# Weight preparation of experts 1 to 5 reordered in a chunked-attention, MoE and dense-MoE kernel

## Chip, cores and metric

The program runs on 1 core of one Trainium2 chip. The metric is device microseconds of one execution of the whole program, from its first to its last instruction. TensorE (PE in the profile) multiplies, VectorE (DVE), ScalarE (ACT) and GpSimd (POOL) do the element-wise work, SyncE (SP) issues most DMAs. Each engine takes its own instructions strictly in the order in which they were written; engines meet only at semaphores.

## What is computed

Three layers follow each other. Only the second, a top-1 mixture of experts, is touched by the change.

```python
attn_out = _attn_ref(**attn_kwargs)              # softmax(q k^T) v within chunks of 64
x = attn_out.transpose(0, 2, 1, 3).reshape(2304, 512)
x = _moe_ref(x=x, **moe_kwargs)                  # each token goes to one of 8 experts
return _moe2_ref(x=x, **moe2_kwargs)             # every token through 8 experts, weighted

# _moe_ref, per expert e, for the tokens routed to it (at most 576):
h = np.maximum(disp[e] @ w1[e], 0.0)             # w1[e] is 512 x 1024
y = h @ w2[e]                                    # w2[e] is 1024 x 512
out[i] = gate_w[i] * y[...]
```

## The kernel before

All matrices are split into two f16 parts, high and low, and each product is three f16 products: high by high, low by high, high by low. So a weight matrix must be prepared before it is used. For each expert that is, for w1 (called a, `nm == "a"`) and w2 (called b):

- **load**: four DMAs into a staging tile (`sta`, `stb`; two of each, used in turn by odd and even experts);
- **statistics** (`w_stat`): four quarters, by ScalarE squares with a running sum for a (line 168), by VectorE maxima for b (line 170);
- **total** (`w_scale`, line 177): one small matmul on TensorE over the partitions, which needs all four quarters;
- **scale** (`w_scale2`): some tiny VectorE instructions that turn the total into a power of two;
- **split** (`w_split`): four quarters each. ScalarE writes the high part (lines 246, 254). The low part comes from VectorE (line 255), or, for two quarters of b, from GpSimd in two steps (lines 247 and 248).

The experts of the first mixture run one after the other, x = 0 to 7. While expert x multiplies, the matrices of y = x + 1 get totals, scales and splits, and those of x + 2 get their loads and statistics. Nothing schedules this at run time: the order is written by hand. `blocks` runs one expert for up to 256 tokens:

- the first product in four groups of 24 matmuls (`first_product`, line 355). Behind each group, `hidden` takes it out of PSUM: ScalarE writes `hh` (line 360), VectorE writes `hl` (line 361). The groups take three PSUM banks in turn, so the fourth group waits until `hl` of the first is written;
- then two rows t = 0 and 1 (128 tokens each) of the second product, 24 matmuls each (line 975). Behind each, the **row finish**: ScalarE square (979), VectorE scale (89 to 92), ScalarE high part (985), VectorE low part (986) and factor (991), and two DMAs (990, 994).

`sites` is a list of six lists of steps. The first four stand behind the four groups, the fifth behind row 0's finish, the sixth behind row 1's finish. `behind` puts a step ahead of matmul step kk of a row (each of the 8 steps has 3 matmuls); at `(0, KF)`, behind row 0's last matmul, stands `late_turn`, which transposes 256 more tokens. After `blocks`, one or two **further blocks** of 128 tokens run, where the count of the expert is over 256 or over 384. In this input expert 2 has two, experts 3 and 6 have one, experts 1, 4 and 5 have none.

In the kernel before, expert 1 alone uses a late order: first total behind the third group, second total at kk = 4 of row 0, splits of b behind row 0's finish. Experts 2 to 6 make both totals and scales behind the first group and spread the eight splits over the four groups. In all of them the statistics of x + 2 (`stats`) stand in the fifth site, ahead of row 1's finish.

Of the kernel before, what the change touches and what calls it, by code (L numbers as in the profile page):

```python
# [30 lines left out]
def kernel(ctx, tc, q, k, v, w_gate, w1, w2, capacity, w2_gate, w21, w22, out):  # L31
# [3 lines left out]
    E, _, F = w1.shape  # L35
# [4 lines left out]
    KF = F // 128  # L40
# [109 lines left out]
    def w_load(x, nm, h, nh=2, behind_vector=False):  # L150
        if h == 0:
            w_new(x, nm)
        m = mats[x, nm]
        c = m.kk // nh
        if behind_vector:
            nc.vector.memset(m.st[:, h * c, 0:1], 0.0)
        nc.sync.dma_start(out=m.st[:, h * c:(h + 1) * c, :],
                          in_=m.src[h * c * 128:(h + 1) * c * 128, :].rearrange("(k p) n -> p k n", p=128))
# [145 lines left out]
    for i in range(NS):  # L304
        r, done = [], 0
        while done < 256:
            b, s = divmod(i * 256 + done, S)
# [600 lines left out]
    with ExitStack() as cctx:  # L908
# [19 lines left out]
        def turn_dma(rows):  # L928
            xT = cp.tile([128, 2 * KD, 256], F16, tag="xT", name="xT", bufs=2)
            for n, (idx, kg, xg) in enumerate(rows):  # L930
                nc.sync.dma_start_transpose(out=xT[:, :, n * 128:(n + 1) * 128], in_=xg)
            return xT, rows
# [70 lines left out]
        def load(x, nm, *hs):  # L1003
            return [lambda h=h: w_load(x, nm, h, 4, x == 2) for h in hs]
# [13 lines left out]
        def tokens(x, *ts):  # L1018
            return [gidx[:, x, t:t + 1] for t in ts]
# [74 lines left out]
        for x in range(E):  # L1094
            y = x + 1

            def skip(b):
                tc.mark_branch_hint_location(f"{b}{x}", rc > {"m": 256, "n": 384}[b], engines=[mybir.EngineType.PE])

            def count(of, counts=reg_i):  # L1100
                return nc.values_load(counts[0:1, of:of + 1], min_val=0, max_val=N)

            def next_count():
                if y < E:
                    counted_next.append(count(y))

            counted_next = []
            if x > 0:
                rc = rc_next
            rb = nc.values_load(reg_i[0:1, E + x:E + x + 1], engines=[mybir.EngineType.SP], min_val=0, max_val=N)  # L1110

            def rank(t):
                return nc.s_assert_within(rb + t * 128, 0, N + 128,
                                          skip_runtime_bounds_check_because="a block starts at most 128 past the last token")

            def ranks(t0):
                return lambda t: rb if t0 + t == 0 else rank(t0 + t)

            def rows_ahead():
                return gather(tokens(y, 2, 3)) if y < E else None, gather(tokens(y + 1, 0, 1)) if y + 1 < E else None  # L1120

            late_cur = late
            if x > 0:
                for f in load(x + 2, "b", 0, 1) if x + 2 < E else ():
                    f()
                cur, pre = pre, turn_dma(rows) if y < E else None
                late, rows = rows_ahead()
            if x == E - 1:
                with tc.If(rc <= N - SB):
                    heads(nc.sync)  # L1130

            if y < E:
                for nm in "ab":
                    w_alloc(y, nm)
                sp = [lambda h=h, nm=nm: w_split(y, nm, h, 4, 2 * (nm == "b" and h > 1)) for h, nm in
                      (((0, "a"), (2, "b"), (1, "a"), (2, "a"), (3, "b"), (3, "a"), (0, "b"), (1, "b")) if x > 1 else
                       ((0, "a"), (1, "a"), (2, "a"), (3, "a"), (2, "b"), (3, "b"), (0, "b"), (1, "b")))]
                sc = [lambda f=f, nm=nm: f(y, nm) for f in (w_scale, w_scale2) for nm in "ab"]
                steps = sc + sp
                counts = (6, 2, 2, 2)  # L1140
            else:
                w_alloc(E, "a")
                wsum = stage2.tile([128, 4, 4, 2, 128], F32, tag="stb", name="wsum")
                wsums += [wsum[:, i] for i in range(4)]
                for q in range(4):
                    w_quad(E, "a", q, 0)
                steps = [lambda f=f: f(E, "a") for f in (w_scale, w_scale2)] + [
                    lambda q=q, i=i: w_quad(E, "a", q, i) for q in range(4) for i in (1, 2)]
                counts = 4, 2, 2, 2
            sites = []  # L1150
            for n in counts:
                sites.append(steps[:n])
                steps = steps[n:]
            assert not steps
            second_sc, second_sp = [], []
            if x == 1:
                sites = [kept_stats[0:1], kept_stats[1:2], [sc[0], sc[2], kept_stats[2], sp[0]], [*sp[1:4], kept_stats[3]]]
                second_sc, second_sp = [sc[1], sc[3]], sp[4:]
            if 0 < x < E - 2:
                sites[1] += load(x + 2, "b", 2, 3)  # L1160
            later = load(x + 3, "a", 0, 1, 2, 3) if x + 3 <= E else []
            stats = []
            for h in range(4):
                if x + 2 <= E:
                    stats.append(lambda h=h: w_stat(x + 2, "a", h, True))
                if x + 2 < E:
                    stats.append(lambda h=h: w_stat(x + 2, "b", h, False))
                elif x == E - 1:
                    sites[h].append(lambda h=h: w_stat(E, "b", h, True))
            nxt = []  # L1170

            def late_turn():
                if x > 0:
                    nxt.append(turn(late_cur, "xTc", "p"))
                    return
                turn_into(e_xT, late_cur, "y")
                for j in range(2):
                    nc.vector.tensor_copy(l_kg[:, j:j + 1], l_rows[j][:, DM:DM + 1])
                nxt.append((e_xT, late_cur))

            if x == 0:
                ahead = []
                every = [f for part in sites for f in part]
                la, lb = load(2, "a", 0, 1, 2, 3), load(2, "b", 0, 1, 2, 3)
                pre_next = turn_dma(rows)
                for f in [every[0], every[2], every[4], every[5]]:
                    f()
                blocks(x, pre, 2, ranks(0), [[*la, lambda: ahead.append(rows_ahead())], lb],
                       True, behind={(0, KF): late_turn})
                pre = pre_next  # L1190
                late, rows = ahead[0]
            else:
                sites += [second_sp + later[:2] + stats if x != E - 2 else load(E, "b", 0, 1, 2, 3) + stats, later[2:]]
                sites[3].append(lambda: skip("m"))
                sites[4].append(next_count)
                blocks(x, cur, 2, ranks(0), sites, True,
                       behind={(0, 4): lambda: [f() for f in second_sc], (0, KF): late_turn})
            late_t, late_r = nxt[0]

            def further(t, sites=()):  # L1200
                blocks(x, (late_t[:, :, (t - 2) * 128:(t - 1) * 128], late_r[t - 2:t - 1]), 1, lambda _: rank(t), sites)

            if x == 0:
                blocks(x, nxt[0], 2, ranks(2), [
                    [lambda: more.append(count(0, e_any)), next_stats[0]], [next_stats[1]], next_stats[2:], [next_count],
                    every[9:],
                    [lambda: tc.mark_branch_hint_location("r", more[0] > 512, engines=[mybir.EngineType.PE]), *later, *stats[0::2]]],
                    behind={(0, 3): lambda: (every[1](), every[3]()), (0, 4): every[6], (0, 5): every[7], (0, 6): every[8]})
                kept_stats = [lambda h=h: w_stat(2, "b", h, False) for h in range(4)]
            else:  # L1210
                with tc.If(rc > 256, label=f"m{x}"):
                    further(2, [[lambda: skip("n")], [], []])
                    with tc.If(rc > 384, label=f"n{x}"):
                        further(3)
            if x == 0:
                with tc.If(more[0] > 512, label="r"):
                    whole()
            if y < E:
                rc_next = counted_next[0]
            else:  # L1220
                with tc.If(rc > N - SB):
                    heads(nc.gpsimd)
# [524 lines left out]
```

## Time and profile before

| | us |
|---|---|
| median of 3 runs | 1748.15 |
| lowest and highest | 1746.42, 1748.84 |
| the profiled execution | 1746.32 |
| span in its profile | 1744.6 |
| experts 1 to 6 within the span | 161.7 to 360.8 |

The profiled execution lies 1.83 us below the median and 1.72 us above its span. The first mixture is about an eighth of the span; the attention lies ahead of it and the second mixture, over two thirds of the span, behind it. The page gives the busy time of each engine; tables by stretch show it per expert, and the waits and timelines show what each engine waited for and when. Times in the timelines count from the start of the span.

### The profile page before, as it was taken

How to read it: one execution, taken by the hardware profiler on the slowest of the kernel's cores; microseconds unless marked ns; L12 is line 12 of the kernel's file. 1: busy time of each engine (PE TensorE's matmuls, PEld its weight loads, DVE VectorE, ACT ScalarE, POOL GpSimd, SP SyncE). 2: the span in 40 equal slices, each digit the busy share in tenths (PEclk: the TensorE clock that was granted, in tenths of full speed). 3: DMA queues.
4: the chain of work that ended last, by engine and by line, in shares of the span. 5: the costliest groups of instructions: out<-in, count | busy, mean ns of one | idle time of the engine just before them, and what ended most of it. 6: DMA issues, size and time to landing. Idle time of an engine off the chain costs nothing.

```text
span 1744.6 us, 33605 instructions
## 1 busy us (share of the span) xinstructions
PE 1695.6 (97%) x13323; PEld 1233.2 (71%) x13323; DVE 1191.8 (68%) x2313; ACT 946.9 (54%) x1795; POOL 715.7 (41%) x758
## 2 busy tenths in 40 slices
PE   8999799989999999999999999999999999999998
PEld 7876466666545577777777777777777777777776
DVE  6886767856567766786677767667766686677554
ACT  6866656764445654665355545555644565364431
POOL 2225544632021333553355444453534543454433
PEclk9999899999999999999999999999999999999999
DMA  9948868845253313242233224223323141323201
GB/s 223 238 137 248 234 162 187 222 116 140 82 148 107 136 62 133 64 175 71 105 116 131 99 95 151 106 85 112 127 92 133 64 171 47 134 64 127 91 35 49
DMA packets 140766, 219.08 MB, mean 126 GB/s; under 512 B 62656, under 2 KB 81120, under 8 KB 140592
## 3 DMA queue, kind: packets, MB, share of 16 engines
q1 hardware_dynamic: 135440, 200.00, 36.6%
q0 software_dynamic: 5152, 16.72, 3.6%
q8 instruction: 114, 1.87, 0.4%
q14 instruction: 60, 0.49, 0.1%
HBM read 167.56 MB, written 41.91 MB: 120 GB/s over the span
## 4 chain that ended last, share of the span: by engine, by line
PE 66%; DVE 6%; ACT 2%; issue 1%; DMA 1%; POOL 1%; SPq 1%; POOLq 0%; DVEq 0%; ACTq 0%
PE p_m L1437 35%; PE p_m L1533 27%; PE p_m L1581 4%; DVE wall L297 3%; ACT wall L296 1%; DVE acc L1504 1%; DMA wb_d<-wall 1%; SPq L1272 1%; PE p_m L1325 0%; DVE xsum L1286 0%; ACT eh L1442 0%; POOL out_dram L1515 0%; DMA x<-x_d 0%; DVE el L1445 0%; ACT tq L1477 0%
## 5 line engine op out<-in xcount | busy, mean ns | idle before, releaser
L1437 PE MATMUL p_m<-x,wall 128*128 128x384 f16 x4032 | 666.9, 326 | 6.0 <-ACT tq L1477 5.1
L1437 PEld LDWEIGHTS <-wall 128*128 128x128 f16 x4032 | 394.1, 98 | 263.4 <-issue 8.8
L1533 PE MATMUL p_m<-wall,eh 128*128 128x256 f16 x3528 | 580.3, 273 | 0.0
L1449 POOL TENSOR_TENSOR el<-tq,eh 128x384 f16<-128x384 f32 x336 | 347.2, 1061 | 560.1 <-ACT eh L1442 559.8
L1533 PE MATMUL p_m<-wall,el 128*128 128x256 f16 x1764 | 480.8, 273 | 0.0
L1442 ACT ACTIVATE eh<-tq 128x384 f16<-128x384 f32 x540 | 274.1, 522 | 189.8 <-DVE tq L1455 101.4
L1533 PEld LDWEIGHTS <-eh 128*128 128x128 f16 x3528 | 344.3, 98 | 44.4
L1504 DVE SCALAR_TENSOR_TENSOR acc<-p_m,cf,acc 128x256 f32<-128x256 f32 (+1 forms) x378 | 175.6, 521 | 130.3 <-PE p_m L1533 129.8
L1452 DVE TENSOR_TENSOR tq<-p_m,tq 128x384 f32<-128x384 f32 x288 | 158.5, 556 | 125.7 <-PE p_m L1437 124.6
L1533 PEld LDWEIGHTS <-el 128*128 128x128 f16 x1764 | 172.6, 98 | 19.9
L1445 DVE SCALAR_TENSOR_TENSOR el<-tq,eh 128x384 f16<-128x384 f32 x204 | 175.1, 860 | 10.0 <-ACT eh L1442 8.6
L1455 DVE SCALAR_TENSOR_TENSOR tq<-tq 128x384 f32<-128x384 f32 x252 | 133.2, 553 | 2.9
L355 PEld LDWEIGHTS <-wall 128*128 128x128 f16 x1248 | 107.2, 99 | 19.6 <-issue 5.4
L1477 ACT COPY tq<-p_m 128x384 f32<-128x384 f32 x96 | 45.7, 476 | 110.6 <-PE p_m L1437 108.2
L247 POOL TENSOR_SCALAR stb<-stb,wsb 128x1024 f32<-128x1024 f32 x16 | 52.7, 3291 | 81.2 <-DVE tq L1452 46.8
L1581 PE MATMUL p_m<-wall,eh 128*128 128x512 f16 x288 | 85.6, 379 | 0.0
L275 POOL TENSOR_TENSOR tq<-stb 128x256 f32<-128x256 f32 x56 | 48.7, 870 | 82.2 <-DVE wsumsq L184 58.9
L296 ACT ACTIVATE wall<-stb,wsb 128x256 f16<-128x256 f32 (+1 forms) x56 | 31.3, 605 | 93.3 <-DMA wb_d<-wall 67.9
L1490 ACT ACTIVATE tq<-tq 128x384 f32<-128x384 f32 x84 | 43.9, 522 | 70.0 <-DVE tq L1452 70.0
L355 PE MATMUL p_p<-xT,wall 128*128 128x256 f16 x672 | 77.6, 276 | 3.6 <-DMA rk_d<-rkt 1.2
L275 POOL TENSOR_TENSOR tq<-sta 128x256 f32<-128x256 f32 x56 | 43.5, 777 | 83.3 <-DVE wall L297 48.6
L297 DVE SCALAR_TENSOR_TENSOR wall<-stb,wsb,wall 128x256 f16<-128x256 f32 (+1 forms) x56 | 38.5, 698 | 48.3 <-ACT wall L296 45.8
(288 smaller groups left out, 2106.6 us busy)
## 6 DMA issues: line engine op xcount, KB each, us to landing
x<-xt_d SPq DMA_DIRECT2D x147, 384.0 KB
wb_d<-wall SPq DMA_DIRECT2D x20, 896.0 KB
wall<-wb_d SPq DMA_DIRECT2D x20, 896.0 KB
sta<-in_moe_w_dram SPq DMA_DIRECT2D x32, 512.0 KB
stb<-in_moe_w_dram SPq DMA_DIRECT2D x32, 512.0 KB
sta<-in_moe_w_dram SPq DMA_DIRECT2D x16, 1024.0 KB
stb<-in_moe_w_dram SPq DMA_DIRECT2D x16, 1024.0 KB
xt_d<-x SPq DMA_DIRECT2D x21, 384.0 KB
```

Source lines behind the costliest of these rows:

```text
L275: nc.gpsimd.tensor_tensor(out=at(o), in0=at(u), in1=at(v), op=op)
L297: nc.vector.scalar_tensor_tensor(out=o[:, cs, 1], in0=src, scalar=m.s, in1=o[:, cs, 0], op0=ALU.mult, op1=ALU.subtract)
L355: nc.tensor.matmul(p[:, f4, :], lhsT=w[:, kk, f * 128:(f + 1) * 128], rhs=xT[:, lo + kk, 0:W], start=(n == 0), stop=(n == 3 * KD - 1))
L1437: nc.tensor.matmul(p, lhsT=wt[:, w, lw, kk, :], rhs=xt[:, lx, kk, :], start=first and n == 0, stop=n == 5, skip_group_check=not first)
L1442: nc.scalar.activation(out=hs[op][0][:, q, :], in_=src, func=AF.Relu if op in (A11, A12, A22) or plain else AF.Copy)
L1445: nc.vector.scalar_tensor_tensor(out=hs[op][1][:, q, :], in0=src, scalar=0.0, in1=hs[op][0][:, q, :], op0=ALU.max, op1=ALU.subtract)
L1449: nc.gpsimd.tensor_tensor(out=hs[op][1][:, q, :], in0=src, in1=hs[op][0][:, q, :], op=ALU.subtract)
L1452: nc.vector.tensor_tensor(out=o, in0=a, in1=b, op=ALU.add)
L1455: nc.vector.scalar_tensor_tensor(out=o, in0=a, scalar=0.0, in1=b, op0=ALU.max, op1=op)
L1504: nc.vector.scalar_tensor_tensor(out=acc[:, j, cols], in0=y, scalar=coefs[x][:, j:j + 1], in1=acc[:, j, cols], op0=ALU.mult, op1=ALU.add)
L1533: nc.tensor.matmul(bk.t[:, cols], lhsT=hs[op][lh][:, q, t * 128:(t + 1) * 128], rhs=b.q[q][:, w, lw, :], start=m in (1, 5) and q == 0 and ...
L1581: nc.tensor.matmul(y.t, lhsT=h[:, kk % 4, c * 128:(c + 1) * 128], rhs=w[:, kk, :], start=(n == 0), stop=(n == 3 * KF - 1))
```

## The change

For experts 1 to 5 (`slow`) one order now holds. Maxima that expert 1 has left over, the first total and its scale stand behind the third group. All four splits of a stand behind the fourth. The second total and its scale stand ahead of step kk = 6 of row 0 (for expert 1 it was kk = 4). The four splits of b stand behind row 0's finish, and the statistics of x + 2 move from there to behind row 1's finish. Expert 6 keeps the old order. The splits of b are also written in the order 2, 3, 0, 1, as expert 1 had it.

```diff
-                      (((0, "a"), (2, "b"), (1, "a"), (2, "a"), (3, "b"), (3, "a"), (0, "b"), (1, "b")) if x > 1 else
+                      (((0, "a"), (2, "b"), (1, "a"), (2, "a"), (3, "b"), (3, "a"), (0, "b"), (1, "b")) if x > 5 else
                        ((0, "a"), (1, "a"), (2, "a"), (3, "a"), (2, "b"), (3, "b"), (0, "b"), (1, "b")))]
...
-            if x == 1:
-                sites = [kept_stats[0:1], kept_stats[1:2], [sc[0], sc[2], kept_stats[2], sp[0]], [*sp[1:4], kept_stats[3]]]
+            slow = 0 < x < 6
+            if slow:
+                kept = kept_stats if x == 1 else []
+                sites = [kept[0:1], kept[1:2], [sc[0], sc[2], *kept[2:4]], sp[0:4]]
                 second_sc, second_sp = [sc[1], sc[3]], sp[4:]
...
-                sites += [second_sp + later[:2] + stats if x != E - 2 else load(E, "b", 0, 1, 2, 3) + stats, later[2:]]
+                sites += ([second_sp + later[:2], later[2:] + stats] if slow else
+                          [later[:2] + stats if x != E - 2 else load(E, "b", 0, 1, 2, 3) + stats, later[2:]])
...
-                       behind={(0, 4): lambda: [f() for f in second_sc], (0, KF): late_turn})
+                       behind={(0, 6): lambda: [f() for f in second_sc], (0, KF): late_turn})
```

**VectorE, expert 1**, first product (`hl` closes a group, `wmxb` is a maximum of b of expert 2, `wall<-sta` a split of a). Before:

```order
L361 SCALAR_TENSOR_TENSOR hl<-p_p,hh 128x512
L205 TENSOR_REDUCE wmma<-p_sum 128x1
L89 TENSOR_SCALAR wh<-wmma 128x1
L90 TENSOR_SCALAR wsa<-wh 128x1
L92 TENSOR_SCALAR wia<-wh 128x1
L170 TENSOR_REDUCE wmxb<-stb_2338 128x1
L255 SCALAR_TENSOR_TENSOR wall<-sta_2297,wsa,wall 128x1024
L361 SCALAR_TENSOR_TENSOR hl<-p_p,hh 128x512
L255 SCALAR_TENSOR_TENSOR wall<-sta_2297,wsa,wall 128x1024 x3
L170 TENSOR_REDUCE wmxb<-stb_2338 128x1
L205 TENSOR_REDUCE wmmb<-p_sum 128x1
```

After:

```order
L361 SCALAR_TENSOR_TENSOR hl<-p_p,hh 128x512
L205 TENSOR_REDUCE wmma<-p_sum 128x1
L89 TENSOR_SCALAR wh<-wmma 128x1
L90 TENSOR_SCALAR wsa<-wh 128x1
L92 TENSOR_SCALAR wia<-wh 128x1
L170 TENSOR_REDUCE wmxb<-stb_2338 128x1 x2
L361 SCALAR_TENSOR_TENSOR hl<-p_p,hh 128x512
L255 SCALAR_TENSOR_TENSOR wall<-sta_2297,wsa,wall 128x1024 x4
L205 TENSOR_REDUCE wmmb<-p_sum 128x1
```

The last maximum moved from behind all four splits to ahead of the last `hl`.

**ScalarE, expert 2**, from row 0's finish to the further block (`w_2_3598<-stb` splits b of expert 3, `wsq` squares a of expert 4, the branch decides on the further block, `hh` behind it belongs to that block). Before:

```order
L979 ACTIVATE sq_3806,ssq_3807<-p_y 128x512
L985 ACTIVATE row_3815<-p_y,x2s 128x2x256
L168 ACTIVATE wsq,wmxa<-sta_3204 128x1024 x4
L1101 TENSOR_LOAD reg_i
L979 ACTIVATE sq_3876,ssq_3877<-p_y 128x512
L985 ACTIVATE row_3885<-p_y,x2s 128x2x256
L1211 COMPARE_AND_BRANCH
L360 ACTIVATE hh<-p_p 128x4x128 x2
```

After:

```order
L979 ACTIVATE sq_3796,ssq_3797<-p_y 128x512
L985 ACTIVATE row_3805<-p_y,x2s 128x2x256
L246 ACTIVATE w_2_3598<-stb_2964,wsb 128x1024 x2
L254 ACTIVATE w_2_3598<-stb_2964,wsb 128x1024 x2
L1101 TENSOR_LOAD reg_i
L979 ACTIVATE sq_3864,ssq_3865<-p_y 128x512
L985 ACTIVATE row_3873<-p_y,x2s 128x2x256
L168 ACTIVATE wsq,wmxa<-sta_3204 128x1024 x4
L1214 COMPARE_AND_BRANCH
L360 ACTIVATE hh<-p_p 128x4x128 x2
```

The four splits of b came in between the two row finishes, and the four squares now stand between row 1's finish and the further block's `hh`.

**VectorE, expert 5**, from the end of row 0's finish to the branch (`wmxb` is of expert 7, the pair at line 255 splits b of expert 6). Before:

```order
L991 SCALAR_TENSOR_TENSOR rkt<-xg,x2i,iw 128x1
L170 TENSOR_REDUCE wmxb<-stb_5432 128x1 x4
L1101 TENSOR_LOAD reg_i
L89 TENSOR_SCALAR x2h<-ssq_5724 128x1
L90 TENSOR_SCALAR x2s<-x2h 128x1
L92 TENSOR_SCALAR x2i<-x2h 128x1
L986 SCALAR_TENSOR_TENSOR row_5732<-p_y,x2s,row_5732 128x2x256
L991 SCALAR_TENSOR_TENSOR rkt<-xg,x2i,iw 128x1
L1211 COMPARE_AND_BRANCH
```

After:

```order
L991 SCALAR_TENSOR_TENSOR rkt<-xg,x2i,iw 128x1
L255 SCALAR_TENSOR_TENSOR wall<-stb_4815,wsb,wall 128x1024 x2
L1101 TENSOR_LOAD reg_i
L89 TENSOR_SCALAR x2h<-ssq_5712 128x1
L90 TENSOR_SCALAR x2s<-x2h 128x1
L92 TENSOR_SCALAR x2i<-x2h 128x1
L986 SCALAR_TENSOR_TENSOR row_5720<-p_y,x2s,row_5720 128x2x256
L991 SCALAR_TENSOR_TENSOR rkt<-xg,x2i,iw 128x1
L170 TENSOR_REDUCE wmxb<-stb_5432 128x1 x4
L1214 COMPARE_AND_BRANCH
```

The maxima of expert 7 moved behind row 1's finish, with a pair of splits ahead of it; expert 6, which comes next, still asks for both totals of expert 7 behind its first group.

## Rows read from the trace of the kernel before

**Rows 1.** The page: busy time of each engine, share of the span, instructions.

```profile
PE 1695.6 (97%) x13323; PEld 1233.2 (71%) x13323; DVE 1191.8 (68%) x2313; ACT 946.9 (54%) x1795; POOL 715.7 (41%) x758
```

**Rows 2.** Stretches: length, then busy PE, PEld, DVE, ACT, POOL; clock, DMA, GB/s.

```profile
161.70:193.50 31.80, 24.49 (x164) 15.90 (x164) 18.15 (x36) 17.44 (x28) 9.70 (x9) 0.89 0.92 256
193.50:223.80 30.30, 24.48 (x164) 16.58 (x165) 26.93 (x39) 21.45 (x33) 27.66 (x17) 0.89 0.74 204
245.50:267.60 22.10, 22.10 (x165) 15.34 (x164) 17.21 (x34) 16.76 (x25) 16.18 (x10) 1.00 0.70 168
```

**Rows 3.** Waits of PE, 145 to 380 us: total us, times, longest.

```profile
PE p_sum L177 <- DVE wmxb L170: 6.3, 1, 6.3
PE p_sum L177 <- DVE x2h L89: 3.4, 2, 2.9
PE p_sum L177 <- ACT wsq L168: 3.2, 2, 2.9
```

**Rows 4.** Stretches of 2 us behind the 6.3 us wait, columns as in rows 2.

```profile
182.00:184.00 2.00, 1.74 (x6) 0.91 (x7) 1.05 (x7) 0.00 (x0) 0.00 (x0) 0.50 1.04 389
184.00:186.00 2.00, 2.00 (x6) 0.70 (x5) 0.00 (x0) 0.00 (x0) 0.00 (x0) 0.50 1.28 262
```

**Rows 5.** Timeline of PE, experts 2 and 5: start, duration, instruction, idle before.

```profile
202.93 9.84 PE L355 MATMUL p_p<-xT,wall 128*128 128x256 f16 x72
217.78 1.06 PE L340 MATMUL p_t<-id,xg 128*128 128x128 f16 x16
...
304.43 8.02 PE L355 MATMUL p_p<-xT,wall 128*128 128x256 f16 x72
```

**Rows 6.** Timeline of VectorE, expert 1 and the start of expert 2.

```profile
177.41 3.67 DVE L255 SCALAR_TENSOR_TENSOR wall<-sta,wsa,wall 128x1024 f16<-128x1024 f32 x3
...
183.71 0.16 DVE L213 TENSOR_TENSOR iw<-wia,wib 128x1 f32<-128x1 f32 x1
...
193.55 4.36 DVE L255 SCALAR_TENSOR_TENSOR wall<-stb,wsb,wall 128x1024 f16<-128x1024 f32 x2 [2.23 <-ACT wall L254]
197.84 4.59 DVE L170 TENSOR_REDUCE wmxb<-stb 128x1 f32<-128x1024 f32 x4
...
203.43 0.75 DVE L986 SCALAR_TENSOR_TENSOR row<-p_y,x2s,row 128x512 f16<-128x512 f32 x1 [0.69 <-ACTq L1211]
...
205.11 0.69 DVE L361 SCALAR_TENSOR_TENSOR hl<-p_p,hh 128x512 f16<-128x512 f32 x1 [0.80 <-ACT hh L360]
```

**Rows 7.** Timeline of ScalarE behind row 0's finish of expert 1.

```profile
190.31 2.18 ACT L246 ACTIVATE wall<-stb,wsb 128x1024 f16<-128x1024 f32 x2
...
194.46 1.05 ACT L168 ACTIVATE wsq<-sta 128x1024 bf16<-128x1024 f32 x1
...
199.05 0.58 ACT L979 ACTIVATE sq<-p_y 128x512 bf16<-128x512 f32 x1
```

**Rows 8.** Timelines of PE and ScalarE, expert 3 and its further block.

```profile
261.56 1.06 PE L340 MATMUL p_t<-id,xg 128*128 128x128 f16 x16
...
267.63 5.52 PE L355 MATMUL p_p<-xTc,wall 128*128 128x128 f16 x96
...
264.87 1.05 ACT L168 ACTIVATE wsq<-sta 128x1024 bf16<-128x1024 f32 x1
```

**Rows 9.** Timelines: splits of b on VectorE beside the two steps of GpSimd.

```profile
293.38 2.73 DVE L255 SCALAR_TENSOR_TENSOR w<-stb,wsb,w 128x1024 f16<-128x1024 f32 x2
...
291.76 3.81 POOL L247 TENSOR_SCALAR stb<-stb,wsb 128x1024 f32<-128x1024 f32 x1
...
316.82 4.34 DVE L255 SCALAR_TENSOR_TENSOR wall<-stb,wsb,wall 128x1024 f16<-128x1024 f32 x2
...
317.04 3.04 POOL L248 TENSOR_TENSOR wall<-stb,wall 128x1024 f16<-128x1024 f32 x1
```

**Rows 10.** Timeline of SP: the transposed tokens for expert 2.

```profile
180.06 6.16 SPq L931 DMA_TRANSPOSE xT<-xg  x2
```

**Rows 11.** Timeline of PE: the first total in expert 6.

```profile
327.43 0.39 PE L177 MATMUL p_sum<-wmxa,ones 128*128 128x4 f32 x2 [0.29 <-ACT wsq L168]
```

## The prediction

> **What bounds the kernel now.** I read the page first: TensorE is busy 97% of the span [rows 1], so time can be won only where it waits, and any new wait costs its length. The table by expert shows where. Expert 3's first 256 tokens take 22.1 us with TensorE busy throughout; expert 1 takes 31.8 us with 24.5 busy, expert 2 30.3 us with 24.5 busy, and in both the mean clock is 0.89 [rows 2]. So about 18 us are there to be won, all in experts 1 and 2, and experts 3 to 6 hold next to nothing. The list of waits names the causes: one wait of 6.3 us for a maximum, and two of 2.9 us for squares and maxima (with two short ones of the same kind in expert 6) [rows 3]. Each was paid for twice: behind the 6.3 us the granted clock was 0.50, the lower level of 1.2 GHz, for some 4 us of matmuls [rows 4], which lost about 2.0 us; behind the pair of 2.9 us, 72 matmuls took 9.84 us where expert 5 needs 8.02 [rows 5], a loss of 1.8.
>
> **A chain that the change makes general.** What stood in expert 1 alone, splits of b behind row 0's finish, now stands in five experts, with the statistics behind row 1's finish. Expert 1 of the trace prices it. Call T the time at which ScalarE has written row 0's high part (190.3). ScalarE then makes four high parts until T + 4.15 (190.31 to 194.46) [rows 7]. VectorE's two splits end at 197.9, T + 7.6 [rows 6]. In the new order row 1's finish is next: from the end of the maxima (202.43) to the end of the row's low part (204.18) it took 1.75 us [rows 6], so T + 9.35; ScalarE's share of it ends some 0.75 earlier, at T + 8.6. Then come four squares (194.46 to 199.05, 4.6 us [rows 7]) until T + 13.2, and four maxima (4.6 us [rows 6]) until T + 13.95. Only behind these stands `hl` (0.69 [rows 6]) of the next block, at T + 14.65. Before the change, in experts 2 to 5, no split lay in this stretch.
>
> TensorE reaches its needs sooner. Let R be the end of row 0's matmuls. Expert 3 shows R = 261.56 and T = 264.87, so T = R + 3.3; transposes and row 1 end at R + 6.1, and a further block's first product at 273.15, R + 11.6 [rows 8]. An expert that follows starts at about R + 6.5; with a group at 8.02 / 3 = 2.67 us [rows 5], its first group ends at R + 9.2 and its third at R + 14.5.
>
> **The terms, in order.**
>
> *Expert 1.* The last two maxima now stand ahead of the four splits of a (1.2 us each [rows 6]). The second total at kk = 6 finds them done: the maximum that ended the wait no longer stands behind the splits. Gain 6.3 plus 2.0 of low clock, 8.3.
>
> *Expert 2, to the end of row 0.* Expert 1's R moves forward by 8.3, but VectorE must still do its four splits (177.4 to 182.3 at 1.22 each) and the second scale, which ended at 183.87 before [rows 6] and does so, or a little earlier, now. The copies of the transposed tokens (about 0.8) and the first 1.0 of the row finish follow, so T is still about 185.2. Expert 2's first `hl` comes at T + 14.65, 199.9; its fourth group then ends at 202.5, and row 0 (about 5.2 us, the 6.07 of [rows 8] without the transposes) at 207.7, or about 208.5 if the clock is low for part of it. Before it was 217.8 [rows 5]. Gain so far 9.3. When the tokens of expert 2 arrive hardly matters: their transposes are issued until 186.2 [rows 10], and the fourth group is held anyway.
>
> *Expert 2, further block.* The splits of a start later than in expert 3, so here T = R + 4.2. The block's first product is ready at R + 11.6, its `hl` at R + 18.85: 7.3 us of waiting. I add 2.0 for the clock, since 6.3 us of idleness cost that. With 0.3 us of small waits gone, loss 9.0. This returns the gain: expert 3 starts where it did, near 245.5.
>
> *Expert 3, further block.* T = R + 3.3, `hl` at R + 17.95, wait 6.4, clock 2.0: loss 8.4.
>
> *Expert 5, behind 4.* The first total, behind the third group, is reached at R + 14.5 and finds the squares at R + 16.5: wait 2.0 to 2.4. The fourth group needs `hl` at R + 17.95: 1.6 more. As with the pair of 2.9 us, I take most of a clock loss, 2.0, and subtract 0.5 of old waits. Loss 5.5.
>
> *Expert 6, behind 5.* Expert 6 still asks for both totals behind its first group, at R + 9.2. Expert 5's start was held, so T = R + 4.2, and the squares end at R + 17.4, the maxima some 0.75 later. Wait 8.8 in all, clock 2.0, less 0.8 of waits that were there (one of them [rows 11]): loss 10.0.
>
> *Cost-free edits.* The work is the same, so nothing is added to an engine. GpSimd's two splits start at T + 1.1 and take 6.85 us each (3.81 and 3.04 [rows 9]), so they end at T + 8 and T + 14.8, which is R + 18.1. The next expert's row 0 reads the last at its step 6, at R + 6.5 + 10.7 + 3.9 = R + 21.1, or later if that expert waits. Without this cover of 3 us the second product would wait for what is missing. SP's loads of b wait longer for the staging tile, but their maxima come an expert later.
>
> Sum: -9.3 + 9.0 + 8.4 + 5.5 + 10.0 = +23.6. Expert 6 ends that much later and the second mixture shifts with it. On the profiled execution (1746.3) this gives 1769.9, on the median of the runs (1748.15, 1.8 above) 1771.7; I say 1771.
>
> **Unknown prices.** First, the clock. Two events lost 2.0 and 1.8 [rows 4, 5]. I take 2.0 four times; the low bound is no loss at all, minus 8.0, and less than that is excluded, since a granted clock of 1.00 is the full 2.4 GHz. Second, the pair of splits on VectorE. It took 2.73 us while GpSimd ran its scalar step and 4.34 while the two-tensor step ran [rows 9]; expert 1, in the very order that becomes general, took 4.36 [rows 6]. I take that; the low bound is 1.6 us less in each of four waits, minus 6.5. Third, the arrival of expert 2's tokens, between 186.2 and 193.5 (where expert 2 started without waiting for them): from nothing to 3.5 us more.
>
> **Rivals.**
>
> *Shorter waits, still slower.* If the clock does not fall (minus 8.0), or the splits take the low price (minus 6.5), or both, the sum is +9 to +17: 1757 to 1765. For it: the trace has only two long waits to learn from. Against: both show the low clock, and the splits at the full price.
>
> *Faster.* The gains of experts 1 and 2 stand (9.3) and nothing is returned, because the chain from T to `hl` is hidden under TensorE's further blocks and groups. This mechanism has its place at the further block of expert 2 and its point of decision in the chain's length: TensorE arrives at about T + 7.5 there, T + 8.3 in expert 3, T + 5 at expert 6's totals. At 5 us less than my 14.65, about 9.7, the waits fall to some 2 us each with little clock loss, and the sum is zero; below that it is faster, down to 1748 - 9 = 1739. For it: experts 1 and 2 did pay for late maxima. Against: the four statistics alone are 4.6 us on each engine and the pair of splits 4.36, in a row on VectorE.
>
> *No change.* The further block returns the gain of expert 2, and the later waits stay below 2 us: 1745 to 1751. It needs the same short chain.
>
> *More than that.* The staging tile of b is free about 12 us later, SP waits for it and holds back what stands behind, the next maxima wait for data: 5 to 10 us more, 1776 to 1782. Against it: the load has half an expert of slack.
>
> *A lock between VectorE and GpSimd.* VectorE's splits were stretched beside GpSimd's two-tensor step (4.34 the pair) and not beside its scalar step (2.73) [rows 9]. If both steps excluded a split entirely, VectorE would wait for each GpSimd step to end; one pair would end about 1.3 us later, in four waits some +5, 1776. The Trainium skill, page "SBUF — State Buffer", section "SBUF: two separate sides", states it so: a VectorE instruction with two SBUF inputs and a GpSimd instruction that reads SBUF exclude each other for the whole instruction, and the second to issue fully blocks. By that rule the time would be 1776; the rows of the scalar step speak against it here, those of the two-tensor step for some of it.
>
> **How the numbers follow.** Forecast, 1766 to 1777: 0.70. Shorter waits: 0.12. More: 0.05. Lock: 0.05. Faster: 0.05. No change: 0.03. The range leaves out the two last and the outer ends of the others: 1761 to 1777, rounded up to 1778 for the lock. A measurement of this kernel tells about 0.2%, 3.5 us, from no change. Only two cases lie below 1751.6: faster 0.05, same 0.03, slower 0.92.
>
> **What would show it.** Right: the 6.3 us wait in expert 1 is gone, row 0 of expert 2 ends near 208, and waits of 6 to 8 us appear in the further blocks of experts 2 and 3 (TensorE for `hl` or `hh`), some 4 us in the start of expert 5 and 8 to 9 us at the first total in expert 6, each with a clock of 0.50 around it; experts 3 and 4 start without a wait. Wrong: further blocks without waits, or the time of expert 6's totals below 3 us; then the chain behind T is shorter than 14.65 us. If the waits stand and the clock does not fall, the second term of each was mis-sized.

## The result, and the profile after

| | us |
|---|---|
| before, median of 4 runs | 1748.49 (1746.42 to 1749.26) |
| after, median of 4 runs | 1765.46 (1763.34 to 1767.61) |
| ratio after / before | 1.0099, 95% interval 1.0081 to 1.0116 |
| span of the profiled run after | 1761.6 |

The changed kernel is slower by 17 us, 1%. The forecast was 1771, with a range of 1761 to 1778: the side and the range hold, the size was 5.5 us too large.

The page shows hardly a difference. Its first part after, to be held against [rows 1] (busy time, share of the span, instructions):

```profile
PE 1697.7 (96%) x13323; PEld 1233.3 (70%) x13323; DVE 1193.6 (68%) x2313; ACT 947.3 (54%) x1795; POOL 709.4 (40%) x758
```

The same number of instructions, and 2 us more of busy TensorE, in a span that is 17.0 longer: some 15 us of the 17 are idle time of TensorE. The timeline of PE after says where. Columns: start, duration, instruction, and in brackets the idle time ahead with what ended it. Only the starts of stages and the waits are shown:

```profile
160.48 8.02 PE L355 MATMUL p_p<-xT,wall 128*128 128x256 f16 x72 [0.30 <-DMA x_d<-row]
...
188.77 10.30 PE L355 MATMUL p_p<-xT,wall 128*128 128x256 f16 x72 [5.31 <-DMA xT<-xg]
...
206.98 1.06 PE L340 MATMUL p_t<-id,xg 128*128 128x128 f16 x16
...
224.52 1.03 PE L975 MATMUL p_y<-wall,hh 128*128 128x512 f16 x2 [5.94 <-ACT hh L360]
...
241.81 8.02 PE L355 MATMUL p_p<-xT,wall 128*128 128x256 f16 x72
...
275.29 1.03 PE L975 MATMUL p_y<-w,hh 128*128 128x512 f16 x2 [5.95 <-ACT hh L360]
...
282.96 8.02 PE L355 MATMUL p_p<-xT,wall 128*128 128x256 f16 x72 [0.55 <-PEq L1216]
...
305.43 8.02 PE L355 MATMUL p_p<-xT,wall 128*128 128x256 f16 x72 [0.30 <-PEq L1214]
315.94 0.39 PE L177 MATMUL p_sum<-wmxa,ones 128*128 128x4 f32 x2 [2.50 <-ACTq L1214]
318.28 5.16 PE L355 MATMUL p_p<-xT,wall 128*128 128x256 f16 x24 [1.95 <-DVE hl L361]
...
335.12 2.78 PE L355 MATMUL p_p<-xT,wall 128*128 128x256 f16 x24 [0.30 <-PEq L1214]
345.64 0.59 PE L177 MATMUL p_sum<-wmxa,ones 128*128 128x4 f32 x2 [7.74 <-ACTq L1214]
...
346.92 9.74 PE L355 MATMUL p_p<-xT,wall 128*128 128x256 f16 x72
...
367.76 5.52 PE L355 MATMUL p_p<-xTc,wall 128*128 128x128 f16 x96
...
379.72 2.78 PE L355 MATMUL p_p<-xT,wall 128*128 128x256 f16 x24 [0.93 <-DMA rk_d<-rkt]
```

The experts begin at 160.48, 188.77, 241.81, 282.96, 305.43, 335.12 and 379.72. The waits of the old experts 1 and 2 [rows 3] are gone. Six new ones have come. Five stand in the stages that the prediction named: the further blocks of experts 2 and 3 (5.94 and 5.95), the first total and the fourth group of expert 5 (2.50 and 1.95), the first total of expert 6 (7.74). The sixth, 5.31 for the tokens of expert 2, the prediction had left with its unknown prices, from nothing to 3.5 us. The releaser `ACTq` is ScalarE's sequencer; what ScalarE did last ahead of the total are the four squares. All the stages with these waits show the low clock: expert 2's start, the two further blocks, experts 5 and 6. The stretches of after (length; busy PE, PEld, DVE, ACT, POOL; granted clock, DMA share, GB/s):

```profile
190.00:192.00 2.00, 2.00 (x11) 1.44 (x10) 1.27 (x5) 0.88 (x2) 2.00 (x1) 0.50 1.04 384
...
222.00:226.00 4.00, 1.48 (x4) 0.39 (x5) 4.00 (x5) 2.92 (x6) 3.56 (x5) 0.50 0.65 43
...
272.00:278.00 6.00, 2.71 (x7) 0.79 (x8) 4.79 (x6) 3.66 (x8) 4.23 (x4) 0.50 0.66 125
318.00:322.00 4.00, 3.72 (x18) 2.68 (x18) 1.86 (x7) 0.48 (x1) 2.64 (x5) 0.50 0.98 388
342.00:350.00 8.00, 4.11 (x19) 3.15 (x20) 6.72 (x16) 5.69 (x10) 5.16 (x6) 0.50 0.70 164
```

Expert by expert, the lengths of the stages in the two profiles (before the starts are 161.71, 245.54, 278.89, 301.45, 324.37 and 360.89 for experts 1, 3, 4, 5, 6, 7; expert 2's row 0 ends at 217.78 [rows 5]; expert 6's further block begins at 348.31):

| stage | before | after | difference | forecast |
|---|---|---|---|---|
| expert 1 to the end of row 0 of expert 2 | 56.07 | 46.50 | -9.6 | -9.3 |
| from there to expert 3, with the further block | 27.76 | 34.83 | +7.1 | +9.0 |
| expert 3 | 33.35 | 41.15 | +7.8 | +8.4 |
| expert 4 | 22.56 | 22.47 | -0.1 | 0 |
| expert 5 | 22.92 | 29.69 | +6.8 | +5.5 |
| expert 6 to its further block | 23.94 | 32.64 | +8.7 | +10.0 |
| its further block | 12.58 | 11.96 | -0.6 | 0 |
| sum | | | +20.1 | +23.6 |
| the attention ahead of expert 1 | 161.71 | 160.48 | -1.2 | 0 |
| the passage into the second mixture | | | -2.0 | 0 |

The passage: expert 7 starts 18.83 later in the second profile, and behind the first matmuls of the second mixture (399.42 before, 416.25 after) 16.83 remain. The sum less 1.2 and 2.0 is 16.9 of the 17.0. From there to the end of the span the distance hardly changes (16.83 to 17.0).

### The profile page after: what moved, and what is told of

Its sections match the earlier page's. It is cut to its first block, busy times and chain, and to the rows that moved or that the text cites. A ratio compares the mean times of both kernels' runs of the same rounds, so it can differ in the third digit from the quotient of the medians.

```text
span 1761.6 us, 33612 instructions
## 1 busy us (share of the span) xinstructions
PE 1697.7 (96%) x13323; PEld 1233.3 (70%) x13323; DVE 1193.6 (68%) x2313; ACT 947.3 (54%) x1795; POOL 709.4 (40%) x758
## 4 chain that ended last, share of the span: by engine, by line
PE 66%; DVE 6%; ACT 2%; issue 1%; DMA 1%; POOL 1%; SPq 1%; POOLq 0%; DVEq 0%; ACTq 0%
PE p_m L1440 35%; PE p_m L1536 27%; PE p_m L1584 4%; DVE wall L297 3%; ACT wall L296 1%; DVE acc L1507 1%; DMA wb_d<-wall 1%; SPq L1275 1%; DVE xsum L1289 0%; PE p_m L1328 0%; ACT eh L1445 0%; DMA x<-x_d 0%; POOL out_dram L1518 0%; DVE el L1448 0%; ACT tq L1480 0%
## 5 line engine op out<-in xcount | busy, mean ns | idle before, releaser
L355 PE MATMUL p_p<-xT,wall 128*128 128x256 f16 x672 | 81.9, 286 | 10.3 <-DMA xT<-xg 5.3
```

The costliest lines, as they stand in the source:

```text
L355: nc.tensor.matmul(p[:, f4, :], lhsT=w[:, kk, f * 128:(f + 1) * 128], rhs=xT[:, lo + kk, 0:W], start=(n == 0), stop=(n == 3 * KD - 1))
```

## Experiments

All are compared with the kernel before on the same chip: median 1747.86 (9 runs) for the first four, 1747.31 (9 runs) for the last four. Intervals are 95%.

**Expert 1 alone.** Start from the kernel before; only expert 1 gets the new places of its maxima and of the second total.

```diff
-                sites = [kept_stats[0:1], kept_stats[1:2], [sc[0], sc[2], kept_stats[2], sp[0]], [*sp[1:4], kept_stats[3]]]
+                sites = [kept_stats[0:1], kept_stats[1:2], [sc[0], sc[2], *kept_stats[2:4]], sp[0:4]]
...
-                       behind={(0, 4): lambda: [f() for f in second_sc], (0, KF): late_turn})
+                       behind={(0, 6): lambda: [f() for f in second_sc], (0, KF): late_turn})
```

> Kernel before with only expert 1's maxima moved ahead of its four splits and its second total at kk = 6; statistics stay ahead of row 1's finish, experts 2 to 6 keep their old order. Theory (the late splits and statistics of experts 2 to 5 cost the time, expert 1's maxima alone gain): expert 1's wait of 6.3 us goes with its low clock, expert 2 then waits some 4 us for its tokens or its totals, sum about -5 us, 1743. Rival (the gain of expert 1 is taken back in expert 2 whatever follows, since VectorE is the bound of both): within 2 us of before, 1747 to 1750.

1741.54 us, ratio 0.9965 (0.9952 to 0.9979): faster than both kernels, as the theory said, which gave 1743. So the part of the change that the forecast put down as a gain is one, and the new order in experts 2 to 5 costs about 24 us (1765.5 - 1741.5; the statistics of expert 1, which stay in place here, are part of it). Its PE timeline at the start of expert 2, and its SP timeline ahead of that:

```profile
193.32 5.28 PE L355 MATMUL p_p<-xT,wall 128*128 128x256 f16 x24 [7.13 <-DMA xT<-xg]
...
182.88 0.91 SPq L157 DMA_DIRECT2D stb<-in_moe_w_dram  x2
183.88 7.28 SPq L931 DMA_TRANSPOSE xT<-xg  x2
```

Row 0 of expert 1 no longer waits, and the next thing that is late is the tokens of expert 2, by 7.13 us where some 4 were expected: they are transposed behind two weight loads on SP's queue.

**Statistics back.** The changed kernel, with the statistics in front of row 1's finish again, as they stood before.

```diff
-                sites += ([second_sp + later[:2], later[2:] + stats] if slow else
+                sites += ([second_sp + later[:2] + stats, later[2:]] if slow else
```

> Changed kernel with the statistics put back ahead of row 1's finish in experts 1 to 5; the splits of b stay behind row 0's finish. Theory (late splits of b are the cause; the chain from row 0's finish to the next block's first hh is as long in either order): the waits in the further blocks of experts 2 and 3 stay near 6 us, expert 5 waits 4 us on hl, expert 6 a little less than in the changed kernel; 1762 to 1766. Rival (the statistics behind row 1's finish are the cause): the waits vanish, and the time is near the one of expert 1's edit alone, 1743 to 1748.

1765.11 us, ratio 1.0104 (1.0089 to 1.0120), the same as the changed kernel and where the theory put it. Its timeline of PE, in the further block of expert 2 (expert 3's waits the same 5.88 us) and at the starts of experts 5 and 6:

```profile
225.40 1.03 PE L975 MATMUL p_y<-wall,hh 128*128 128x512 f16 x2 [5.88 <-ACT hh L360]
...
319.07 5.12 PE L355 MATMUL p_p<-xT,wall 128*128 128x256 f16 x24 [4.71 <-DVE hl L361]
...
342.08 0.59 PE L177 MATMUL p_sum<-wmxa,ones 128*128 128x4 f32 x2 [3.42 <-ACT wsq L168]
345.36 0.59 PE L177 MATMUL p_sum<-wmxb,ones 128*128 128x4 f32 x2 [2.69 <-DVE x2h L89]
```

Where the statistics stand relative to row 1's finish makes no difference to the end of the chain: both must be done before the next `hh`. With late splits they are late either way.

**Splits early.** The changed kernel, with the totals and splits of experts 2 to 5 in their old early places; the statistics stay behind row 1's finish.

```diff
-                       (((0, "a"), (2, "b"), (1, "a"), (2, "a"), (3, "b"), (3, "a"), (0, "b"), (1, "b")) if x > 5 else
+                       (((0, "a"), (2, "b"), (1, "a"), (2, "a"), (3, "b"), (3, "a"), (0, "b"), (1, "b")) if x > 1 else
...
-            slow = 0 < x < 6
+            slow = x == 1
...
-                sites += ([second_sp + later[:2], later[2:] + stats] if slow else
+                sites += ([second_sp + later[:2], later[2:] + stats] if 0 < x < 6 else
```

> Changed kernel with experts 2 to 5 back at the old totals and splits (behind the first group and spread over the four), but with their statistics behind row 1's finish; expert 1 in the new order. Theory: waits in the further blocks fall from 6 to about 1.5 us, but each expert that follows one without a further block waits 3 to 5 us at its first total (experts 2, 5 and 6); 1754 to 1758. Rival (the statistics alone are the cause): waits of 6 us in the further blocks as in the changed kernel, 1763 to 1767.

1756.48 us, ratio 1.0053 (1.0038 to 1.0069), where the theory put it. PE, the further block of expert 2 (expert 3's waits the same 1.64 us), and the first totals of experts 5 and 6 (expert 2's waits 2.87 us):

```profile
228.39 0.61 PE L975 MATMUL p_y<-wall,hh 128*128 128x512 f16 x2 [1.64 <-ACT hh L360]
...
309.15 0.39 PE L177 MATMUL p_sum<-wmxa,ones 128*128 128x4 f32 x2 [3.43 <-ACTq L1214]
...
337.69 0.39 PE L177 MATMUL p_sum<-wmxa,ones 128*128 128x4 f32 x2 [3.43 <-ACTq L1214]
```

The further blocks wait 1.64 instead of 5.9, so the late splits make most of that wait. The first totals, which stand behind the first group again, now pay for statistics that come after row 1. The four corners together. The rows are the places of totals and splits in experts 2 to 5 (expert 1 has its new ones in each); the columns hold for experts 1 to 5:

| | statistics before row 1 | statistics behind row 1 |
|---|---|---|
| splits early | 1741.5 | 1756.5 |
| splits late | 1765.1 | 1765.5 |

Either move alone costs: the late statistics 15 us, the late splits 24. With the splits late, moving the statistics adds nothing; with the statistics late, the splits still add 9.

**Expert 6 late too.** If an expert of the old order pays for the late work of the one ahead, the wait of 7.74 should go when expert 6 takes the new order as well.

```diff
-                       (((0, "a"), (2, "b"), (1, "a"), (2, "a"), (3, "b"), (3, "a"), (0, "b"), (1, "b")) if x > 5 else
+                       (((0, "a"), (2, "b"), (1, "a"), (2, "a"), (3, "b"), (3, "a"), (0, "b"), (1, "b")) if x > 6 else
...
-            slow = 0 < x < 6
+            slow = 0 < x < 7
...
-                sites += ([second_sp + later[:2], later[2:] + stats] if slow else
+                sites += ([second_sp + (later[:2] if x != E - 2 else load(E, "b", 0, 1, 2, 3)), later[2:] + stats] if slow else
```

> Changed kernel with expert 6 in the late order too, so that it asks for its first total behind the third group. Theory (the border between late and old order costs some 5 us): expert 6's wait of 7.7 us at the first total falls to some 3 plus 1.2 for the fourth group, its further block waits 6 us instead of none, which takes a part back; 1760 to 1763. Rival (the border costs nothing, the time is lost to the chain of expert 5 and is waited for somewhere in any case): 1765 to 1768.

1770.02 us, ratio 1.0132 (1.0117 to 1.0148): outside both expectations, slower than the changed kernel. PE of this kernel from expert 6's first total to its further block:

```profile
347.29 0.39 PE L177 MATMUL p_sum<-wmxa,ones 128*128 128x4 f32 x2 [2.26 <-ACTq L1214]
349.62 4.29 PE L355 MATMUL p_p<-xT,wall 128*128 128x256 f16 x24 [1.95 <-DVE hl L361]
...
365.13 5.52 PE L355 MATMUL p_p<-xTc,wall 128*128 128x128 f16 x96
...
376.60 1.04 PE L975 MATMUL p_y<-wall,hh 128*128 128x512 f16 x2 [5.95 <-ACT hh L360]
...
384.57 2.78 PE L355 MATMUL p_p<-xT,wall 128*128 128x256 f16 x24 [0.93 <-ACT sq L979]
```

The wait at the first total fell as the theory had it, 7.74 to 2.26 and 1.95: expert 6 to its further block took 28.1 (365.13 - 337.00) instead of 32.6. But expert 6 has a further block, and that now waits 5.95 at the low clock and takes 19.4 instead of 12.0. The expectation had named this wait of 6 us, but its range did not follow from its own terms: it saved 3.5 at the total and lost 6 behind it, before any low clock, and still came out below the changed kernel. Net +3.0 in expert 6; the low clock in the passage, seen below, adds 1.6. The remaining 1.0 of the 5.6 us by which this profile is longer (span 1767.2 against 1761.6) lies in stages that the edit leaves alone; these differ by up to 1.5 us between the two profiles.

**Expert 5 old.** The border moved the other way: the new order in experts 1 to 4 only.

```diff
-                       (((0, "a"), (2, "b"), (1, "a"), (2, "a"), (3, "b"), (3, "a"), (0, "b"), (1, "b")) if x > 5 else
+                       (((0, "a"), (2, "b"), (1, "a"), (2, "a"), (3, "b"), (3, "a"), (0, "b"), (1, "b")) if x > 4 else
...
-            slow = 0 < x < 6
+            slow = 0 < x < 5
```

> Edit: the changed kernel, with expert 5 back in the old order (experts 1 to 4 stay in the new one). Theory (an expert in the old order behind one in the new order pays at its first total for the statistics and splits that its predecessor left behind, whichever number it has): expert 5's first total waits 7 to 8 us at the low clock and expert 5 is longer by 8.7 than before the change, expert 6 costs what it did before; of 1765.5 the 6.8 that expert 5 pays in the new order go: 1757 to 1761. Rival 1 (the 7.7 us at the first total are expert 6's own, since it alone issues its weight loads behind its first row): expert 5 takes its old time, expert 6 still waits 7 to 8: also 1757 to 1761, but with the wait in the other place. Rival 2 (both pay): 1765 to 1768.

1760.99 us, ratio 1.0085 (1.0070 to 1.0101). PE, experts 5 and 6:

```profile
308.05 2.78 PE L355 MATMUL p_p<-xT,wall 128*128 128x256 f16 x24 [0.30 <-PEq L1214]
318.57 0.59 PE L177 MATMUL p_sum<-wmxa,ones 128*128 128x4 f32 x2 [7.73 <-ACTq L1214]
...
340.94 2.78 PE L355 MATMUL p_p<-xT,wall 128*128 128x256 f16 x24 [0.30 <-PEq L1214]
343.55 0.28 PE L177 MATMUL p_sum<-wmxa,ones 128*128 128x4 f32 x2
```

The wait of 7.73 moved from expert 6 to expert 5, which took 32.9 (340.94 - 308.05), 10.0 more than before the change where 8.7 was expected; expert 6's totals wait for nothing. So the wait belongs to the border between the orders, not to expert 6 and its loads. The time lies at the upper end of what that theory gave.

**Three attempts on expert 2's tokens**, on top of expert 1 alone. The first asks for expert 2's totals one group later (behind the second group, not the first) and spreads its splits over the two groups behind:

```diff
+            if x == 2:
+                sites = [[], [*sc, *sp[0:2]], sp[2:5], sp[5:8]]
```

> Edit: expert 1 alone in the new order (1741.5 us, 0.9965), and in expert 2 both totals and both scale steps go behind the second group of the first product, the splits behind the groups after it. Theory (in the new expert 1 order the only idle time left in expert 2's first half is the 7.13 us in which TensorE waits for the transposed tokens; its first total, at 198.39, waits for nothing): totals that are asked for sooner are not the thing waited for, 1741 to 1743. Rival (the statistics of expert 3's weights that now stand behind each other in expert 1 reach into expert 2, and a total asked for one group later is a wait hidden in the clock): 1738 to 1740.

(What the text there calls "sooner" is one group later than in the kernel with expert 1 alone.) 1738.76 us, ratio 0.9957 (0.9944 to 0.9971): where the rival put it, though its interval overlaps that of expert 1 alone. No total waits, in either. From the start of expert 1 to the end of expert 2's row 0 it takes 47.8 us (160.64 to 208.45), against 49.1 (163.20 to 212.26) in expert 1 alone. But its wait for the tokens is 5.38 instead of 7.13, and this wait stands ahead of the steps that the edit moves. It also varies where the code up to it is the same (5.31, 6.47 and 6.36 in the changed kernel, expert 6 late and expert 5 old). So a gain by the edit is not shown. The second issues the transposes of expert 2's tokens before the two loads:

```diff
+                if x == 1:
+                    cur, pre = pre, turn_dma(rows)
                 for f in load(x + 2, "b", 0, 1) if x + 2 < E else ():
                     f()
-                cur, pre = pre, turn_dma(rows) if y < E else None
+                if x > 1:
+                    cur, pre = pre, turn_dma(rows) if y < E else None
```

> Edit: expert 1 alone in the new order, and in expert 1 the two transposes of expert 2's tokens are issued on SP's queue ahead of the two weight loads that stand before them. Theory (the 7.13 us at the start of expert 2 are the queue's order: the loads wait for their staging buffer until 182.88, the transposes follow at 183.88 and take 7.28 us): the wait goes, but the first total of expert 2, which came 7 us after it with nothing to wait for, then waits some 3 us for the statistics, as it does in experts 5 and 6 where statistics stand behind the row: 1735 to 1739. Rival (the wait only moves, since the loads that are now later by 7 us hold up the maxima of expert 3's weights, and the totals of expert 2 wait for all of it): 1740 to 1744.

1741.21 us, ratio 0.9966 (0.9952 to 0.9979), no better than expert 1 alone. Its SP issue, and PE at the start of expert 2:

```profile
174.12 8.69 SPq L931 DMA_TRANSPOSE xT<-xg  x2
...
186.53 4.45 PE L355 MATMUL p_p<-xT,wall 128*128 128x256 f16 x24 [2.69 <-DMA xT<-xg]
...
192.52 0.39 PE L177 MATMUL p_sum<-wmxa,ones 128*128 128x4 f32 x2 [1.54 <-ACT wsq L168]
195.79 0.59 PE L177 MATMUL p_sum<-wmxb,ones 128*128 128x4 f32 x2 [2.89 <-DVE x2h L89]
```

Counted from the start of expert 1 (160.86 here, 163.20 in expert 1 alone), the transposes are issued 7.4 us sooner and take 1.4 longer; the wait for tokens falls by 4.4, and 4.4 come back at the two totals, behind the squares and the maxima. The rival's time was right, 1740 to 1744, and so was its place, the totals, but not its reason: the maxima are not held up by the later loads, since they begin 30.3 us after the start of expert 1 in both kernels (191.15 - 160.86 and 193.50 - 163.20). TensorE merely reaches them sooner: expert 2 is held by two things that end within a few microseconds of each other. Both edits together:

> Edit: the two edits of the runs beside it together. Theory (totals are what expert 2 waits for once its tokens come in time; asked for one group later they find their maxima done): 1 to 2 us under the run with the tokens alone, 1734 to 1737. Rival (totals of expert 2 are not on the path even then): the same as the run with the tokens alone within 1 us.

1739.46 us, ratio 0.9960 (0.9947 to 0.9974), with 3.85 us of waiting for tokens and 2.01 for the second total: 1.8 us under the second attempt, between what theory and rival gave. These three and expert 1 alone are not told apart by these runs: the intervals overlap. All lie under the kernel before by 0.3 to 0.4%.

## Why the prediction was right, and where its sizes were off

**Expert 1 and row 0 of expert 2 (-9.3, measured -9.6): the right size, partly by accident.** The 6.3 us wait and the low clock behind it are gone. But I wrote that the tokens' arrival hardly matters since the fourth group is held by `hl`. In the profile after, TensorE waits 5.31 for the tokens, and its first three groups take 10.30 at the low clock; the fourth stands ready right behind them, at 199.05, and the first `hl` was written at about 198.7 (two from 198.03 in 1.29). The two bounds met within half a microsecond in this profile. That is luck, since the wait for the tokens varied by 1.2 us between kernels with the same code up to there. No run takes the tokens' wait away from the changed kernel itself.

**The chain, T + 14.65: TensorE goes on at T + 13.7 (224.52).** After, in expert 2, ScalarE and then VectorE from T (210.82) to the next block's `hh` and `hl`:

```profile
210.82 2.17 ACT L246 ACTIVATE w<-stb,wsb 128x1024 f16<-128x1024 f32 x2
...
218.72 0.69 ACT L985 ACTIVATE row<-p_y,x2s 128x512 f16<-128x512 f32 x1 [3.07 <-DVE x2s L90]
219.30 1.05 ACT L168 ACTIVATE wsq<-sta 128x1024 bf16<-128x1024 f32 x1
...
223.89 1.07 ACT L360 ACTIVATE hh<-p_p 128x512 f16<-128x512 f32 x2
...
214.07 4.36 DVE L255 SCALAR_TENSOR_TENSOR w<-stb,wsb,w 128x1024 f16<-128x1024 f32 x2 [2.24 <-ACT w L254]
...
220.23 4.59 DVE L170 TENSOR_REDUCE wmxb<-stb 128x1 f32<-128x1024 f32 x4
...
224.74 1.28 DVE L361 SCALAR_TENSOR_TENSOR hl<-p_p,hh 128x512 f16<-128x512 f32 x2
```

Splits end at T + 7.6, squares begin at T + 8.5 (forecast 8.6) and end at T + 13.1 (13.2), the maxima end at T + 14.0 (13.95). The 3.07 us of ScalarE is the knot: row 1's scale stands behind VectorE's pair of splits, and so do ScalarE's squares. The step that was off is the last one: I let the further block wait for `hl`. Its first matmuls need only `hh`, which ScalarE writes at T + 13.1, before VectorE gets to `hl`; the latter is then ready as the next matmuls want it.

**The further blocks (waits 7.3 and 6.4, measured 5.94 and 5.95).** Ending at `hh` takes 0.95 off in both (13.7 instead of 14.65). In expert 2, T was R + 3.8 (210.82 - 206.98), not R + 4.2, which takes another 0.4 off; in expert 3 it was R + 3.85 (261.59 - 257.74), not R + 3.3, which gives 0.5 back. The clock took 1.6 in expert 2, not 2.0: from 224.52 to 231.27 the second product took 6.75 us, where the same one of the block behind it took 5.18 (236.63 to 241.81) at the full clock. In expert 3 it took 1.9 (275.29 to 282.41, 7.12 us). Together +7.1 and +7.8 instead of +9.0 and +8.4.

**Expert 5 (5.5, measured 6.8).** The waits were right in place and nearly in size: 2.50 for the squares (forecast 2.0 to 2.4) and 1.95 for `hl` (1.6). Here the chain does end at `hl`, and later than forecast: even the first `hh` stood idle until VectorE was done with the maxima (316.73), and `hl` followed 0.80 behind it, at 317.53. ScalarE in expert 5:

```profile
316.90 1.57 ACT L360 ACTIVATE hh<-p_p 128x512 f16<-128x512 f32 x3 [1.01 <-DVEq L1214]
```

The low clock took 2.5 instead of 2.0 (the fourth group 5.16 instead of 2.78, the rest at the total), and only 0.2 of old waits went, not 0.5.

**Expert 6 (10.0, measured 8.7).** 7.74 and 0.25 of waiting (the second total) instead of 8.8: the squares end at T + 13.1 and the total follows (345.64, T = 332.43). The 72 matmuls behind it took 9.74 instead of 8.02, 1.7 of low clock. The old waits that went were 1.3 (0.29, 0.46 and 0.51 in the profile before), not 0.8.

**Not in the sum: the passage into the second mixture.** Its first matmuls stood at the low clock in the profile before and at the full clock in the profile after, though the work and the idle time ahead (0.57 and 1.68) are the same. The stretches of 2 us behind that idle time, before and then after:

```profile
388.00:390.00 2.00, 2.00 (x22) 2.00 (x20) 0.93 (x3) 0.48 (x1) 0.00 (x0) 0.50 0.39 132
```

```profile
406.00:408.00 2.00, 1.99 (x30) 1.82 (x31) 1.45 (x3) 0.87 (x3) 0.00 (x0) 1.00 0.39 132
```

22 matmuls against 30 in the same time. Of the 2.0 us of the passage 1.6 come from this (from 385.20 before and 403.67 after, 18.47 apart, to where 16.83 remain); the other 0.4 are short waits in expert 7. In the ten profiles of this study the clock there was low in three (before, expert 6 late too, tokens before weights).

On the profiled executions the forecast was 1769.9 and the time 1763.34, 6.6 less: 3.5 of it is the sum (20.1 instead of 23.6, in which one term too small, expert 5's, stands against others that were too large), 2.0 the passage and 1.2 the attention, which the change doesn't touch.

**The rivals.** "Shorter waits" described the direction of the miss, but not by its mechanism: the clock did fall, and the pair of splits took 4.36 as forecast. "Faster" had put its point of decision at a chain of 9.7 us; it measured 13 to 14. The lock between VectorE and GpSimd was not a rival in truth: the price of 4.36 came from expert 1 [rows 6], where the two engines' steps already stood side by side, so whatever they do to each other was in it, and adding to it counted that twice. In the profile after, the pair took 4.36 again. Its second split, GpSimd's two-tensor step beside it, and the same step later with no split beside it:

```profile
215.27 3.16 DVE L255 SCALAR_TENSOR_TENSOR w<-stb,wsb,w 128x1024 f16<-128x1024 f32 x1
```

```profile
214.99 2.36 POOL L248 TENSOR_TENSOR w<-stb,w 128x1024 f16<-128x1024 f32 x1
...
221.22 2.13 POOL L248 TENSOR_TENSOR w<-stb,w 128x1024 f16<-128x1024 f32 x1
```

The pair's first split took 1.29 us, until 215.35. GpSimd's step began 0.36 before that and took 0.23 longer than it does alone. The second split began under the step, ended 1.08 after it (218.43 and 217.35) and took 3.16 in all, 1.9 more than the first. These rows fit an exclusion of one by the other: 1.28 for the first split, 2.00 from its end to the end of the step, and 1.08 more are the 4.36. GpSimd's spans are rough in a profile, so this is a fit and not a proof. Beside the scalar step, which ran until 295.57, a pair took 2.73 [rows 9], little more than two splits alone (three took 3.67 [rows 6]). The rule of the Trainium skill, page "SBUF — State Buffer", section "SBUF: two separate sides", is that of an exclusion for the whole instruction; the rows of the two-tensor step agree with it, those of the scalar step do not. GpSimd's two splits ended at T + 12.5 here (223.35), not at T + 14.8, and nothing waited for them.

## What to carry over

Where a matrix is prepared while another multiplies, take each step's chain up to the next thing that TensorE waits for, and compare it with the work that TensorE has in that stretch: preparation that was free behind the groups of a large block was waited for once it stood behind the row finishes, by a small block that follows or by the next expert's first total. An order that cures a wait in one expert should be tried there alone first; here that alone was worth 0.35%, and made general it cost 24 us more than that. When a wait goes, look at what else ends within a few microseconds of it, since that is the bound that comes next. Stages with the same code differed by up to 1.5 us between two profiles, so a difference of that size in one stage is not yet the work of an edit.

## What was not expected of the hardware

That a long idle stretch of TensorE costs more than its length was forecast, at 2.0 us each; in the profile after it was 1.6 us more behind 5.94 us of waiting, 1.9 behind 5.95, 1.7 behind 7.74, 2.5 behind the pair of 2.50 and 1.95, and 2.3 behind 5.31 (10.30 instead of 8.02 for 72 matmuls), each at a granted clock of 0.50.

What was not expected are the short ones. The same two short idle times of 0.57 and 1.68 us at the passage into the second mixture brought the low clock in three profiles of ten and not in seven, which moves the time by 1.6 us, though the edits leave that place as it is. In expert 2's further block, waits of 1.44 us (expert 1 alone) and 1.77 (its first attempt on the tokens) had the low clock behind them, waits of 1.64 (splits early) and 1.94 (both edits together) the full one. The stretches of 2 us behind the first and the third of these:

```profile
227.00:229.00 2.00, 2.00 (x6) 0.73 (x5) 0.00 (x0) 0.00 (x0) 0.00 (x0) 0.50 0.94 348
```

```profile
230.00:232.00 2.00, 2.00 (x11) 0.94 (x10) 0.00 (x0) 0.00 (x0) 0.00 (x0) 1.00 0.65 133
```

So the length of the wait alone does not decide it. What does stays open.
